# Order of the logit transposes and the third stage's products, and of the high rows' stores, in a long convolution followed by soft mixture-of-experts

## The chip, the cores and the metric

The kernel runs on one core of one Trainium2 chip. The metric is the device time of one execution in microseconds (us), lower being better; where several runs are given, their median is used. Profiles come from one separately profiled execution.

The core has five engines with instruction queues of their own: TensorE (PE in the profile, its weight loads as PEld), VectorE (DVE), ScalarE (ACT), GpSimd (POOL) and SyncE (SP), which here issues nearly all DMA transfers. Each queue is worked off in order; queues wait for each other through semaphores.

## The reference

The input `x` is (8, 5696, 128), the filter `h` is (5696, 128), both float32. The first half is a causal convolution along the 5696 positions, done as a product of Fourier transforms of twice that length:

```python
Xf = np.fft.rfft(x, n=2 * S, axis=1)
Hf = np.fft.rfft(h, n=2 * S, axis=0)
y = np.fft.irfft(Xf * Hf[None], n=2 * S, axis=1)[:, :S, :]
```

The result is taken as 45568 tokens of 128 values. The second half is a soft mixture of experts with 8 experts of 4 slots:

```python
logits = x @ phi                        # (45568, 32)
d = softmax(logits, axis=0)             # dispatch, over the tokens
slot_input = d.T @ x                    # (32, 128)
slot_out[e] = relu(slot_input[e] @ w1[e]) @ w2[e]
c = softmax(logits, axis=1)             # combine, over the slots
out = c @ slot_out                      # (45568, 128)
```

The dispatch softmax runs over all tokens, so no output row can be made before the last token's logits are known; the kernel keeps a running column maximum and rescales a running sum.

## The kernel before

**Transform.** The length is split as 90 x 64 (5696 = 89 x 64), and the filter is treated as a ninth batch, the first one. There are three stages, and between them the data goes to DRAM and comes back in another layout.

- *First stage.* A chunk `c` is four of the 32 column pairs of one batch; a batch has 8 chunks, so there are 72. `load_x` (L184) loads it in two transfers, `fold` (L202) makes its sum and difference on POOL (`comp` 0 and 1), and `first_stage` (L210) multiplies them by a table (L217) into two PSUM banks, which ACT copies to `fst` (L220). SP stores `fst` to the DRAM tensor `f` (L226). The 90 rows of the result are split: `first_low` makes the first 60 for one chunk, two stores of 240 KB; `first_high` makes the last 30 for two chunks at once, in four strips of 32 partitions (strip `o` starts at partition 32 `o`; the order is chunk c-1 comp 0, chunk c-1 comp 1, chunk c comp 0, chunk c comp 1), four stores of 120 KB. `fst` has four buffers.
- *Second stage.* A batch has 12 units. `load_g` (L243) brings one in (`gt`, 512 KB). `stage_b1` (L254) transforms it on PE (L263) into `bt` and multiplies by the filter's spectrum on DVE (L281, L290, giving `yf`). `stage_b2` (L294) transforms back (L305); ACT copies the result to `zst` (L311), and SP stores it to the DRAM tensor `z` (L314). `stage_b2` always works on the unit before the one that `stage_b1` has just done.
- *Third stage.* A pair `T` is two chunks of output; a batch has 4 pairs, so there are 32. `load_pair` (L334) brings it in with five transfers (`zc`, 1.4 MB, one buffer until the tail). `stage_c1` (L348) is a generator with three steps: the first makes two products of four matmuls each (L361, two PSUM banks), ACT copies one (L370) and DVE makes sum and difference with the other (L366, L367). The second makes two more products and copies one to `om` (L374). The third makes the sum and difference again on DVE, and POOL makes the final rows of `y` (L380).

**Experts' front.** For a pair, `stage_c2` transposes `y` (L391), `stage_c3` makes the logits (L400) and copies them to `lt` (L403), and `column_max` (L407) updates the running negative maximum `low` on DVE. `stage_c4` (L425) transposes `lt` on PE (four transposes into one bank, L429), copies the result to `L` (L433) and makes the exponential of `lt` with `low` as the bias (L435), with a second small exponential for rescaling (L440); POOL clears one column (L437), DVE takes the maximum over the slots (L444), and POOL subtracts it (L445). `stage_c5` (L449) transposes the exponentials (L452); `softmax` (L458) and `stage_c6` (L500) finish the combine weights; `dispatch` (L471) adds to the slots' sums.

**Order.** It is written out by hand. A loop runs over time steps `t` from 0 to 80, and in every step the letters of a string are called one after the other; `work_` (L592) says which function a letter stands for. Odd steps use ORDER_E, even steps ORDER_O (in the first nine steps FILL_E and FILL_O) (L566). The engines' queues take the instructions in this order.

In an odd step of ORDER_E: `x` loads a chunk, `X` and `Y` are `first_low` and `first_high`, `f` folds the next chunk, `1` is the first step of `stage_c1` for pair T, `4` is `stage_c4` for pair U = T - 1, `j` and `w` are the second and third step of `stage_c1`, `b` is a unit of the second stage, `5` is `stage_c5` and `s` is `softmax` for U. In an even step of ORDER_O: `z` loads the next pair, `P` loads units, `x`, `X`, `f`, `b` as before, `2`, `3` and `m` are `stage_c2`, `stage_c3` and `column_max` for the pair made in the step before, `6` is `stage_c6`, `d` is `dispatch`.

The first stage ends with step 71. Pair T is in step 27 + 2T, so `stage_c4` first comes in step 29. After step 80 the last pairs follow in straight code (L643 on), then the experts' small products, and last the output (L798 on). This code calls the same functions in an order of its own.

All PSUM banks used by these functions come from `bank()` (L173), a ring of four until the tail: a product can begin when the bank taken four calls earlier has been read.

Of the kernel before, what the change touches and what calls it, by code (L numbers as in the profile page):

```python
# [77 lines left out]
def kernel(  # L78
# [94 lines left out]
    def bank():  # L173
        rings.append(rings.pop(0))
        return rings[-1].tile([P, 512], F32, name="bank", tag="bank")
# [23 lines left out]
    def folded(c, comp):  # L199
        return xf[c % 2 * 2 + comp]  # L200
# [9 lines left out]
    def first_stage(tiles, width):  # L210

        st = apool.tile([P, CH, 2, D], F32, name="fst", tag="fst", bufs=4)
        for G in range(2):
            p = bank()
            for o, (c, comp) in enumerate(tiles):
                k = slice(0, HP) if width == HP else slice(HP, HP + QP)
                nc.tensor.matmul(p[o * width:(o + 1) * width, :], s1[:, comp + G, k],  # L217
                                 folded(c, comp)[:, :, :].rearrange("p n d -> p (n d)"),
                                 start=True, stop=True)
            nc.scalar.activation(st[:, :, G, :],  # L220
                                 p[:, :].rearrange("p (n d) -> p n d", d=D), AF.Copy)
        for o, (c, comp) in enumerate(tiles):
            g, j = divmod(c, NJ)
            n0 = comp * HALF + CH * j
            k0, n = (0, N1A) if width == HP else (N1A, N1 - N1A)
            nc.sync.dma_start(  # L226
                out=fd[g].rearrange("q a r c d -> (q a) (r c d)")[k0:k0 + n, n0 * 2 * D:(n0 + CH) * 2 * D],
                in_=st[o * width:o * width + n, :, :, :].rearrange("k n c d -> k (n c d)"))

    def first_low(c):  # L230
        first_stage([(c, comp) for comp in range(2)], HP)

    def first_high(c):
        first_stage([(c - 1 + i, comp) for i in range(2) for comp in range(2)], QP)
# [328 lines left out]
    for comp in range(2):  # L563
        fold(0, comp)
    wait_b2 = []
    ORDER_E, ORDER_O, FILL_E, FILL_O, XAHEAD = "xXYf14jwb5s", "zPxXfb26db3m", "xYfX14jwb5s", "zPxfXb26db3m", 3  # L566

    for t in range(last_front + 1):
        us = list(units(t))
# [286 lines left out]
```

## Time and profile before

| | |
|---|---|
| time, median of 3 runs | 865.26 us (859.84 to 866.72) |
| the profiled execution | 866.74 us, of which the span is 864.4 us |
| PE busy | 769.7 us (89% of the span) |
| DVE busy | 626.5 us (72%) |
| ACT busy | 437.4 us (51%) |
| POOL busy | 374.8 us (43%) |
| DMA | 271.99 MB, 315 GB/s on average |

The span is the profiled execution from its first to its last instruction. In the profile, L217 is line 217 of the kernel, `bank<-x,s` is what an instruction writes and reads, and the arrow `<-` in a list of waits names what ended an engine's idle time. A matmul's time in the profile includes that of its pipeline, so the sum of single matmuls can be larger than the time they take together: four transposes of 272 ns each are through 0.59 us after they began.

The main loop has a steady part. From about 200 us to 640 us each two steps (one odd, one even) repeat after 20.26 us. Before it, up to 200 us, the third stage is not yet running; between 640 and about 720 us the first stage is over and the loop runs out; then come the last pairs, the experts' products, and from about 800 us the output.

### The profile page before, as it was taken

How to read it: one execution, taken by the hardware profiler on the slowest of the kernel's cores; microseconds unless marked ns; L12 is line 12 of the kernel's file. 1: busy time of each engine (PE TensorE's matmuls, PEld its weight loads, DVE VectorE, ACT ScalarE, POOL GpSimd, SP SyncE). 2: the span in 40 equal slices, each digit the busy share in tenths (PEclk: the TensorE clock that was granted, in tenths of full speed). 3: DMA queues.
4: the chain of work that ended last, by engine and by line, in shares of the span. 5: the costliest groups of instructions: out<-in, count | busy, mean ns of one | idle time of the engine just before them, and what ended most of it. 6: DMA issues, size and time to landing. Idle time of an engine off the chain costs nothing.

```text
span 864.4 us, 20502 instructions
## 1 busy us (share of the span) xinstructions
PE 769.7 (89%) x7796; PEld 374.4 (43%) x7796; DVE 626.5 (72%) x942; ACT 437.4 (51%) x967; POOL 374.8 (43%) x359
## 2 busy tenths in 40 slices
PE   5878888779999999999999999999978878978882
PEld 1222333234444444444444444444444444445882
DVE  3259867658777878887888788877778997973542
ACT  3422344435655655665566556656544545562531
POOL 2133424245556556665566555555533443540000
PEclk9999999989999999999999999999999999997755
DMA  9989999999999999999999999999997797760998
GB/s 294 294 268 308 306 319 342 337 335 331 329 323 343 343 349 318 343 337 340 325 336 345 320 339 330 348 312 335 334 333 264 265 316 277 283 276 8 371 380 327
DMA packets 153243, 271.99 MB, mean 315 GB/s; under 512 B 11878, under 2 KB 110054, under 8 KB 150005
## 3 DMA queue, kind: packets, MB, share of 16 engines
q1 hardware_dynamic: 152571, 270.38, 90.5%
q8 instruction: 62, 1.02, 0.4%
q10 hardware_dynamic: 576, 0.31, 0.1%
q14 instruction: 34, 0.28, 0.1%
HBM read 142.57 MB, written 127.98 MB: 313 GB/s over the span
## 4 chain that ended last, share of the span: by engine, by line
PE 58%; DMA 21%; DVE 12%; SPq 3%; issue 2%; ACT 1%; POOL 1%; DVEq 0%; ACTq 0%; POOLq 0%
PE bank L217 14%; PE bank L361 13%; PE bank L305 8%; PE bt L263 7%; PE bank L391 5%; DMA zc<-z 5%; DMA xc<-in_x_dram 5%; DMA out_dram<-o 5%; PE bank L478 3%; DMA gt<-f 3%; DMA xc<-in_h_dram 2%; DVE yf L290 2%; SPq L342 2%; DVE p L281 2%; DVE bt L281 2%
## 5 line engine op out<-in xcount | busy, mean ns | idle before, releaser
L207 POOL TENSOR_TENSOR x<-xc 128x512 f32<-128x512 f32 x126 | 158.0, 1276 | 245.0 <-PE bank L217 177.0
L217 PE MATMUL bank<-x,s 128*64 128x512 f32 (+1 forms) x1152 | 224.6, 610 | 14.0 <-DVE x L207 9.2
L311 ACT ACTIVATE zst<-bank 128x512 f32<-128x512 f32 (+1 forms) x184 | 98.6, 586 | 184.3 <-PE bank L305 165.1
L220 ACT ACTIVATE fst<-bank 128x512 f32<-128x512 f32 x216 | 127.4, 598 | 106.3 <-PE bank L217 87.6
L281 DVE TENSOR_TENSOR p<-bt,Hi 128x1024 f32<-128x1024 f32 x96 | 111.3, 1160 | 32.7 <-PE bt L263 31.6
L361 PE MATMUL bank<-zc,i 128*64 128x512 f32 x480 | 119.1, 618 | 12.4 <-DMA zc<-z 10.0
L305 PE MATMUL bank<-yf,vt 64*64 64x256 f32 x1440 | 100.8, 387 | 25.7 <-DVE yf L290 25.6
L263 PE MATMUL bt<-gt,wt 64*64 64x256 f32 x1620 | 114.3, 389 | 9.6 <-DMA gt<-f 8.1
L290 DVE TENSOR_TENSOR yf<-bt,p 128x512 f32<-128x512 f32 x192 | 119.4, 663 | 3.3
L217 PEld LDWEIGHTS bank<-x,s 128*64 128x64 f32 (+1 forms) x1152 | 55.8, 124 | 150.3 <-issue 79.9
L281 DVE TENSOR_TENSOR bt<-bt,Hr 128x1024 f32<-128x1024 f32 x96 | 113.0, 1177 | 0.0
L263 PEld LDWEIGHTS bt<-gt,wt 64*64 64x64 f32 x1620 | 54.2, 132 | 84.6 <-issue 33.1
L380 POOL TENSOR_TENSOR y<-y,op 128x512 f32<-128x512 f32 x64 | 77.6, 1212 | 13.4 <-DVE op L366 10.4
L305 PEld LDWEIGHTS bank<-yf,vt 64*64 64x64 f32 x1440 | 56.3, 134 | 57.4 <-issue 23.1
L366 DVE TENSOR_TENSOR y<-bank,y 128x512 f32<-128x512 f32 x32 | 22.1, 692 | 77.3 <-PE bank L361 73.8
L380 POOL TENSOR_TENSOR y<-y,om 128x512 f32<-128x512 f32 x54 | 64.1, 1187 | 2.1
L361 PEld LDWEIGHTS bank<-zc,i 128*64 128x64 f32 x480 | 30.9, 139 | 76.8 <-issue 46.6
L391 PE MATMUL bank<-ident,y 109*128 109x109 f32 x512 | 62.4, 272 | 1.3 <-DVE y L380 1.0
L391 PEld LDWEIGHTS bank<-ident,y 109*128 109x128 f32 x512 | 52.1, 147 | 17.2 <-issue 9.2
L393 ACT ACTIVATE yt<-bank 128x360 f32<-128x360 f32 x128 | 51.0, 490 | 2.4 <-PE bank L391 1.8
L809 PE MATMUL op<-so,cT 32*128 32x128 f32 x704 | 45.9, 379 | 5.7 <-ACT o L818 5.2
L466 POOL TENSOR_TENSOR L<-L,rs 128x512 f32<-128x512 f32 x32 | 33.6, 1051 | 31.1 <-DVE rs L465 20.9
(96 smaller groups left out, 792.0 us busy)
## 6 DMA issues: line engine op xcount, KB each, us to landing
gt<-f SPq DMA_DIRECT2D x99, 512.0 KB
z<-zst SPq DMA_DIRECT2D x88, 512.0 KB
f<-fst SPq DMA_DIRECT2D x144, 240.0 KB
zc<-z SPq DMA_DIRECT2D x30, 1024.0 KB
xc<-in_x_dram SPq DMA_DIRECT2D x64, 320.0 KB
f<-fst SPq DMA_DIRECT2D x144, 120.0 KB
out_dram<-o SPq DMA_DIRECT2D x16, 1024.0 KB
zc<-z SPq DMA_DIRECT2D x90, 128.0 KB
```

The lines of the kernel that those rows point to most:

```text
L207: eng.tensor_tensor(out=folded(c, comp)[:, :, :], in0=t_[:, 0, :, :], in1=t_[:, 1, ::-1, :], op=AL.subtract if comp else AL.add)
L217: nc.tensor.matmul(p[o * width:(o + 1) * width, :], s1[:, comp + G, k], folded(c, comp)[:, :, :].rearrange("p n d -> p (n d)"), start=True ...
L220: nc.scalar.activation(st[:, :, G, :], p[:, :].rearrange("p (n d) -> p n d", d=D), AF.Copy)
L263: nc.tensor.matmul(bt[q * HP:(q + 1) * HP, a, o, :], wt[r, 2 * i + q, :], t_[r, 2 * o + q, :, :].rearrange("p c d -> p (c d)"), start=True ...
L281: nc.vector.tensor_tensor(out=p_, in0=pv, in1=h_, op=AL.mult)
L290: eng.tensor_tensor(out=y_[r, 0:k, c, :], in0=pv[:, :, c, :], in1=pi[r, 0:k, 1 - c, :], op=op_)
L305: nc.tensor.matmul(bz[q][a * HP:(a + 1) * HP, o * 2 * D:(o + 1) * 2 * D], vt[r, i, a, :], y_[r, a * m + o, :, :].rearrange("p c d -> p (c ...
L311: nc.scalar.activation(st[:, 0:m, q, :], bz[q][:, 0:m * 2 * D].rearrange("p (o x) -> p o x", o=m), AF.Copy)
L361: nc.tensor.matmul(p[h_ * HP:(h_ + 1) * HP, :], i1[0:kr, tab, :], t_[0:kr, h_, o, :, q, :], start=True, stop=True)
L380: eng.tensor_tensor(out=part_, in0=part(v, 0), in1=o_[:, :, :], op=sign)
L391: nc.tensor.transpose(p[:, i * TR:(i + 1) * TR], ys[T][0:TR, k * CH + i, 0:D], ident[0:TR, 0:TR])
L393: nc.scalar.activation(yt[:, k * CH:(k + 1) * CH, :, :], of_tokens(p), AF.Copy)
```

## The change

Two lines change.

In `first_stage` the stores of `fst` are issued in a different sequence. The list of strips is sorted by whether the strip's number is odd. For the low rows with two strips this leaves the sequence as it was. For the high rows with four strips it becomes 0, 2, 1, 3, which starts at partitions 0, 64, 32, 96 where it was 0, 32, 64, 96. Each store writes the same bytes to the same place.

In ORDER_E the letters `1` and `4` change places: `stage_c4` of pair U is issued ahead of the first step of `stage_c1` of pair T. The other three strings stay.

```diff
-        for o, (c, comp) in enumerate(tiles):
+        for o, (c, comp) in sorted(enumerate(tiles), key=lambda v: v[0] % 2):
             g, j = divmod(c, NJ)
             n0 = comp * HALF + CH * j
             k0, n = (0, N1A) if width == HP else (N1A, N1 - N1A)
@@
-    ORDER_E, ORDER_O, FILL_E, FILL_O, XAHEAD = "xXYf14jwb5s", "zPxXfb26db3m", "xYfX14jwb5s", "zPxfXb26db3m", 3
+    ORDER_E, ORDER_O, FILL_E, FILL_O, XAHEAD = "xXYf41jwb5s", "zPxXfb26db3m", "xYfX14jwb5s", "zPxfXb26db3m", 3
```

More of the change, by code (lines that the diff above doesn't have):

```diff
@@ L565 @@
     wait_b2 = []
-    ORDER_E, ORDER_O, FILL_E, FILL_O, XAHEAD = "xXYf14jwb5s", "zPxXfb26db3m", "xYfX14jwb5s", "zPxfXb26db3m", 3
+    ORDER_E, ORDER_O, FILL_E, FILL_O, XAHEAD = "xXYf41jwb5s", "zPxXfb26db3m", "xYfX14jwb5s", "zPxXfb26db3m", 3
     for t in range(last_front + 1):
```

## The prediction

> **What bounds the kernel now.** I read the page's slices first, then the stretches, then who TensorE waits for, then single pairs in order of time.
>
> ```profile
> PE   5878888779999999999999999999978878978882
> DMA  9989999999999999999999999999997797760998
> ```
>
> Slices of 21.6 us. From slice 10 to 29 both PE and DMA stand at 9. The table of stretches says how full they are (columns: length, then busy us of each engine, granted clock, DMA share, GB/s):
>
> ```profile
> 100.00:200.00 100.00, 81.11 (x767) 32.86 (x764) 68.00 (x80) 42.51 (x77) 35.41 (x29) 0.95 0.99 332
> 200.00:640.00 440.00, 431.70 (x4462) 201.79 (x4462) 352.67 (x541) 261.91 (x596) 254.18 (x237) 1.00 0.97 334
> 640.00:720.00 80.00, 66.96 (x720) 36.76 (x720) 68.29 (x106) 36.81 (x85) 27.46 (x28) 0.89 0.84 289
> ```
>
> 100 to 200 us is the transfers' stretch (0.99 busy, PE at 81%). 200 to 640 us is PE's: 431.7 of 440 us busy, so 8.3 us is all that any edit can win there without taking PE work away. From 640 us (no first stage left) VectorE carries it, 68.3 of 80 us. What PE waits for between 200 and 650 us (us in total, times, longest):
>
> ```profile
> PE bank L361 <- DMA zc<-z: 5.3, 6, 2.6
> PE bank L305 <- DVE yf L290: 3.5, 6, 1.8
> PE bank L361 <- DMA f<-fst: 1.2, 1, 1.2
> PE bank L361 <- ACT fst L220: 0.9, 1, 0.9
> ```
>
> The waits ahead of L361 are what the first edit aims at. One of them in order of time (start, us, work):
>
> ```profile
> 477.74 3.79 PE L217 MATMUL bank<-x,s 128*64 128x512 f32 x24
> 482.18 1.94 PE L361 MATMUL bank<-zc,i 128*64 128x512 f32 x8 [0.66 <-DMA zc<-z]
> 484.05 0.66 PE L429 MATMUL bank<-ident,lt 128*128 128x128 f32 x4
> 484.64 1.94 PE L361 MATMUL bank<-zc,i 128*64 128x512 f32 x8
> ```
>
> The four transposes behind the products need only `lt`, there since the step before; they take 0.59 us on PE (484.05 to 484.64). Lastly a pair after 640 us, where nothing stands between L400, which makes `lt`, and these transposes:
>
> ```profile
> 664.30 1.94 PE L361 MATMUL bank<-zc,i 128*64 128x512 f32 x8
> 664.63 0.49 ACT L403 ACTIVATE lt<-bank 128x360 f32<-128x360 f32 x1
> ...
> 665.43 0.60 ACT L370 ACTIVATE y<-bank 128x512 f32<-128x512 f32 x1 [0.30 <-PE bank L361]
> 666.17 0.66 PE L429 MATMUL bank<-ident,lt 128*128 128x128 f32 x4
> ...
> 667.76 0.61 ACT L435 ACTIVATE dt<-lt,low 128x360 f32<-128x360 f32 x1 [0.30 <-DVE low L416]
> 667.78 0.69 DVE L366 TENSOR_TENSOR y<-bank,y 128x512 f32<-128x512 f32 x1
> ...
> 670.42 0.69 DVE L367 TENSOR_TENSOR om<-bank,om 128x512 f32<-128x512 f32 x1
> ```
>
> Here L403 runs under the first products, and DVE, not PE, ends last: L305 later waits 2.67 us for `yf`.
>
> **What the Trainium skill says.** (1) "SBUF — State Buffer", section 'Can I just issue two DMAs to hit both halves?': two transfers at once, at partitions 0 and 64, gave +6% over one. (2) "DMA: Bandwidth & Descriptors", 'Rules for kernel authors', says of transfers to disjoint halves "Don't bother — they serialize". The trace agrees as far as it goes: put in order of time, the 4 KB packets of the high stores take 177 ns on average and those of the low stores, whose two transfers already lie in opposite halves, 176 ns. (3) "TensorE: Matmul & The Clock Gate", 'Part 4: PE-mode transpose', gives about 275 ns for a 128x128 transpose in a kernel (bf16). L429 shows 272 ns each, but four overlap to 0.59 us; I use the 0.59.
>
> **Part 1: the order of products and transposes (32 pairs have L429; the 26 that the loop issues change, 22 before 640 us and 4 after; the written-out tail does not).** Nothing is added. On PE the four L429 move ahead of sixteen L361; on ACT L433, L435 and L440 move ahead of L370; on DVE L444 moves ahead of the first L366 and L367. POOL's (L437, L445, then L380) and SP's orders stay. In the ring of four PSUM banks the block's fifth, the last L361's, now waits for L433 and not L370; either is done over a microsecond before.
>
> *While PE is full (22 pairs).* Both orders keep PE 0.59 + 2 x 1.87 = 4.3 us, so without a wait nothing is won. Where `zc` is late, PE does the 0.59 us in the wait. The gaps ahead of L361 are 0.41, 0.68, 0.86, 0.66, 0.35, 0.58 and 1.24 us; of each at most 0.59 is filled: 0.41 + 0.35 + 0.58 + 4 x 0.59 = 3.7 us. Does it stay won? `zc` may simply come at its own time again. After the wait at 400.9 us the transfers run dry (share 0.83 from 411 to 420 us) because SP waits for work that PE paces, so they should move up with it; at 97% I allow four fifths: -2.9 us.
>
> What could eat it is ACT. Count from the start of this block: the last L220 copy ends at 0.81. L433, L435 and L440 follow each other at 0.5 us, so L370 starts near 2.0 and not 1.12, ends at 2.6, when the second L361 bank is full too (2.6 against 2.04). DVE then folds from 2.65 to 4.1. The next fold starts at 4.51 today and waits for the last L361 at 4.39. So 0.4 us of slack is left: cost nothing, with that as its cover.
>
> *The first pair after 640 us.* L361 waits 2.61 us for `zc`, `lt` and `low` being ready (642.9 and 644.4). The transposes, 1.1 us here at a lowered clock, go into the wait: -1.1 us. The block took 6.0 us where others take 4.4, clock granted 0.81 around it; if a shorter idle time avoids that, up to 1 us more, which I don't count.
>
> *The other three.* The transposes must wait for L403: L400's end to L403's end is 0.8 us, plus 0.1, so PE idles 0.9 us (now covered by L361). Behind it, L435 on ACT waits for `low` (3.46 after the first L361 today), then L440, so L370 starts about 4.05 and not 1.13. On DVE, behind the column maximum ending at 3.56: L444 to 4.25, a wait for L370 to 4.65, then four folds of 0.70 us: 7.5 against 6.82 today. So +0.7 us on the chain that ends last, three times: +2.1 us. Bounds: 0 (if a later wait takes it up) and 1.0 each.
>
> **Part 2: the stores.** The same four transfers of 120 KB, in the same place of SP's order, in the sequence of rows 0, 64, 32, 96. Whoever needs the data or the buffer waits for all four, whose bytes go through one queue. From below: the high stores' packets lie 17 ns over the median 159; 36 groups x 120 packets x 17 ns / 16 engines = 4.7 us, if all of that vanished and all of it were on the path. The page's +6% gives an estimate of 4.1 us: groups last some 1.9 us, 36 x 1.9 x 0.06. From above: the low stores, already alternating, are within 1 ns, 0.3 us by the same working; I keep 1 us. I take 0, since the low stores show no advantage.
>
> **Sum.** -2.9 - 1.1 + 2.1 + 0 = -1.9 us. The profiled execution took 866.7 us (span 864.4, 2.3 around it): it would be 864.8. Against the median of the runs, 865.26, that is 863.4. The three runs lie 6.9 us apart, so a measurement of this kernel tells about 1% (8.7 us) from no change, and this isn't.
>
> **The rivals.**
> - *All of it pays* (0.14): the waits are filled whole (-3.7), the clock holds at 645 us (-2.1), the drain's 2.1 us is absorbed, the stores gain the 4.1 us: 865.3 - 9.9 = 855.4. For: 100 to 200 us is bound by transfers. Against: 22 of the 36 groups lie where PE sets the pace, and packets are near their floor already.
> - *The copy in ACT's queue* (0.12): L370 behind L433, L435 and L440 makes L366 and L367 late in the 22 full pairs too. It decides once L370 slips 0.4 us beyond my 2.0. At 0.75 us beyond, 0.35 x 22 = +7.7; the drain at 1.0 each, +3.0; the waits won are lost in it; -1.1 stays: 865.3 + 9.6 = 874.9. For: DVE's `yf` comes just before PE wants it (L305 at 9.67 after the block's start, DVE done at 9.52). Against: ACT is busy 60%, and its times repeat to 0.01 us from pair to pair.
> - *It does not do what it says* (0.14): `zc` comes when the transfers let it, so each wait grows by what was filled. Then -1.1 + 2.1 = +1.0: 866.3.
> - My forecast (0.60): 863.4, 859 to 868 on its own.
>
> **Numbers.** Of the first rival somewhat over half lies beyond 1%, of the second under half: faster 0.08, within 1% 0.87, slower 0.05. The range 857.5 to 870 leaves out the far halves of these two and the outer edge of the runs' own scatter.
>
> **What would show it.** Right: in the list of waits, L361 <- `zc` and `fst` between 200 and 640 us falls from 4.8 to about 1.5 us, PE's busy time there stays, and the period of two steps stays 20.26 us; after 650 us, L429 waits 0.9 us for L403 three times, and the last fold of a pair ends about 0.7 us later after L400. The packets of the high stores keep their 177 ns. Wrong: a period over 20.3 us with DVE's L366 waiting for L370 (second rival); L361's waits as long as before (third); a GB/s over 340 between 100 and 200 us with that stretch shorter by 2 us or more (first). A wait of L305 for `yf` in every pair would break the slack I rely on.

## The result

Over 20 runs of each the changed kernel takes 865.42 us (858.63 to 871.75) and the kernel before 865.84 us (859.7 to 872.31): a ratio of 0.9992, 95% interval 0.9973 to 1.0012, that is -2.3 to +1.0 us. Nothing that can be measured. (The ratios in this document leave out the few executions that fell into the chip's slower state, here one of the changed kernel, so they can differ a little from those of the medians.)

A correction first. The changed kernel has a third difference, which the description and the diff above miss: FILL_O, the order of the even steps 0 to 8, reads `zPxXfb26db3m` and not `zPxfXb26db3m`. There the fold of the next chunk (on DVE in these steps, in step 8 on POOL) and `first_low` (PE, ACT, SP) change places. They use different engines, and with and without this difference every engine gets the same instructions in the same order with the same waits. So it changes nothing that runs, and the two parts treated above are what there is.

### The profile page after: what moved, and what is told of

Its sections match the earlier page's. It is cut to its first block, busy times and chain, and to the rows that moved or that the text cites. A ratio compares the mean times of both kernels' runs of the same rounds, so it can differ in the third digit from the quotient of the medians.

```text
span 863.6 us, 20505 instructions
## 1 busy us (share of the span) xinstructions
PE 764.5 (89%) x7796; PEld 378.0 (44%) x7796; DVE 627.4 (73%) x942; ACT 435.5 (50%) x967; POOL 374.7 (43%) x359
## 4 chain that ended last, share of the span: by engine, by line
PE 54%; DMA 21%; DVE 14%; SPq 4%; issue 2%; ACT 2%; POOL 1%; DVEq 0%; ACTq 0%; POOLq 0%
PE bank L217 12%; PE bank L361 11%; PE bank L305 7%; PE bt L263 7%; PE bank L391 6%; DMA zc<-z 6%; DMA xc<-in_x_dram 5%; DMA out_dram<-o 4%; DMA gt<-f 3%; PE bank L478 3%; DVE yf L290 3%; DVE p L281 2%; DVE bt L281 2%; DMA xc<-in_h_dram 2%; SPq L342 2%
## 5 line engine op out<-in xcount | busy, mean ns | idle before, releaser
L217 PE MATMUL bank<-x,s 128*64 128x512 f32 (+1 forms) x1152 | 224.8, 615 | 10.9 <-DVE x L207 8.3
L361 PE MATMUL bank<-zc,i 128*64 128x512 f32 x480 | 113.4, 614 | 15.1 <-DMA f<-fst 7.7
L263 PE MATMUL bt<-gt,wt 64*64 64x256 f32 x1620 | 113.9, 388 | 12.2 <-DMA gt<-f 10.8
L305 PE MATMUL bank<-yf,vt 64*64 64x256 f32 x1440 | 99.9, 384 | 25.1 <-DVE yf L290 25.0
L217 PEld LDWEIGHTS bank<-x,s 128*64 128x64 f32 (+1 forms) x1152 | 55.7, 124 | 146.7 <-issue 80.9
L263 PEld LDWEIGHTS bt<-gt,wt 64*64 64x64 f32 x1620 | 54.2, 132 | 87.9 <-issue 38.9
L305 PEld LDWEIGHTS bank<-yf,vt 64*64 64x64 f32 x1440 | 56.0, 133 | 56.0 <-issue 20.1
L361 PEld LDWEIGHTS bank<-zc,i 128*64 128x64 f32 x480 | 35.3, 139 | 72.4 <-issue 51.2
L391 PE MATMUL bank<-ident,y 109*128 109x109 f32 x512 | 62.8, 273 | 1.3 <-DVE y L380 1.0
L391 PEld LDWEIGHTS bank<-ident,y 109*128 109x128 f32 x512 | 52.4, 147 | 17.0 <-issue 10.8
L444 DVE TENSOR_REDUCE rm<-L 128x16 f32<-128x512 f32 x32 | 21.9, 685 | 40.8 <-POOL x L207 37.5
```

The lines of the kernel that those rows point to most:

```text
L263: nc.tensor.matmul(bt[q * HP:(q + 1) * HP, a, o, :], wt[r, 2 * i + q, :], t_[r, 2 * o + q, :, :].rearrange("p c d -> p (c d)"), start=True ...
L305: nc.tensor.matmul(bz[q][a * HP:(a + 1) * HP, o * 2 * D:(o + 1) * 2 * D], vt[r, i, a, :], y_[r, a * m + o, :, :].rearrange("p c d -> p (c ...
L361: nc.tensor.matmul(p[h_ * HP:(h_ + 1) * HP, :], i1[0:kr, tab, :], t_[0:kr, h_, o, :, q, :], start=True, stop=True)
L391: nc.tensor.transpose(p[:, i * TR:(i + 1) * TR], ys[T][0:TR, k * CH + i, 0:D], ident[0:TR, 0:TR])
```

## The profile after

The table of stretches of the changed kernel (columns as above: length, busy us of PE, PEld, DVE, ACT, POOL, granted clock, DMA share, GB/s):

```profile
100.00:200.00 100.00, 80.22 (x765) 32.91 (x766) 68.04 (x81) 43.44 (x79) 35.15 (x30) 0.97 0.97 328
200.00:640.00 440.00, 428.24 (x4464) 204.93 (x4464) 354.17 (x541) 259.31 (x594) 253.49 (x235) 1.00 0.97 335
640.00:720.00 80.00, 65.36 (x722) 37.08 (x716) 66.96 (x104) 36.85 (x86) 27.55 (x28) 0.91 0.83 290
```

Between 200 and 640 us PE is busy for 3.5 us less than before (428.2 against 431.7), with as many matmuls (4464 against 4462), and idle for 3.5 us more. The transfers stand at 0.97 as before. What PE waits for in this stretch (us in total, times, longest), first L361 in the kernel before:

```profile
PE bank L361 <- DMA zc<-z: 2.7, 5, 0.7
PE bank L361 <- DMA f<-fst: 1.2, 1, 1.2
PE bank L361 <- ACT fst L220: 0.9, 1, 0.9
```

Then the changed kernel:

```profile
PE bank L305 <- DVE yf L290: 3.5, 6, 1.8
PE bank L361 <- DMA zc<-z: 3.3, 3, 1.7
PE bank L361 <- DMA f<-fst: 2.5, 3, 1.1
PE bank L361 <- ACT dn L440: 1.3, 1, 1.3
PE bank L361 <- ACT L L433: 0.8, 1, 0.8
PE bank L361 <- ACT fst L220: 0.2, 1, 0.2
```

L361 waited 4.8 us before; now it waits 8.1 us, and that after the transposes have filled the first 0.59 us of each gap. (L440 and L433 had ended when the wait ended, and L361 reads nothing of `f`; what these matmuls still lack is `zc`.) One of these waits in order of time:

```profile
477.11 3.79 PE L217 MATMUL bank<-x,s 128*64 128x512 f32 x24
480.83 0.66 PE L429 MATMUL bank<-ident,lt 128*128 128x128 f32 x4
482.28 3.65 PE L361 MATMUL bank<-zc,i 128*64 128x512 f32 x16 [0.79 <-DMA f<-fst]
```

PE comes 0.6 us earlier than before to the end of L217 (480.83 against some 481.5), does the transposes in the gap as forecast, and the products begin at 482.28 where they began at 482.18. `zc` came when it came.

And a pair after 640 us:

```profile
662.88 0.81 PE L400 MATMUL bank<-yt,phi 128*32 128x360 f32 x8
...
663.96 0.49 ACT L403 ACTIVATE lt<-bank 128x360 f32<-128x360 f32 x1
664.50 0.66 PE L429 MATMUL bank<-ident,lt 128*128 128x128 f32 x4 [0.80 <-ACT lt L403]
...
667.09 0.60 ACT L435 ACTIVATE dt<-lt,low 128x360 f32<-128x360 f32 x1 [1.30 <-DVE low L416]
...
667.68 0.58 ACT L370 ACTIVATE y<-bank 128x512 f32<-128x512 f32 x1
...
668.29 0.69 DVE L366 TENSOR_TENSOR y<-bank,y 128x512 f32<-128x512 f32 x1 [0.50 <-ACT y L370]
...
670.34 0.69 DVE L367 TENSOR_TENSOR om<-bank,om 128x512 f32<-128x512 f32 x1
```

The queue of events is the one forecast: L429 waits 0.80 us for L403, L435 waits for `low`, L370 stands behind it, DVE waits for L370. L400 began at 662.88, so the last fold ends 8.15 us after it (671.03); before, it ended 7.55 us after (663.56 to 671.11).

## The experiments

Theory T says that the steady part goes at the pace of the transfers: whatever PE saves, the next wait for `zc` grows by it (the third rival). Theory F says what the forecast said: filled waits stay won, and then something else must have lost them.

**The order alone.** Only the first part of the change:

```diff
-    ORDER_E, ... = "xXYf14jwb5s", ...
+    ORDER_E, ... = "xXYf41jwb5s", ...
```

> Part 1 alone: stage_c4 ahead of the first step of stage_c1 in the odd steps, stores as before. Theory T (transfers pace the steady part, so L361's wait for zc grows by whatever PE saves): a full pair takes 20.10 us and not 20.26, the waits ahead of L361 between 200 and 640 us add up to about 8 us and not 4.8, and the distance from the L361 of step 29 to the last L400 before 645 us stays at 443.5 us within 1 us; time within 0.3% of before. Theory F (the filled waits stay won, as in the forecast, and something else took them away in the changed kernel, the stores being the candidate): that distance falls by 3 us or more and the time by 0.3% or more.

Measured: 865.53 us against 864.84, ratio 0.9996 (0.9972 to 1.0019). A full pair takes 20.10 to 20.11 us, the distance is 444.8 us (before 443.5, changed kernel 443.1). So no stores are needed to lose the gain; F fails here. The distance is 1.4 us more than before and not within 1 us as T had it. It scatters by that much from one execution to another: in the profiled executions with the full load it is 443.5 us twice with the old order (before, and the stores alone below) and 443.1, 444.8 and 443.4 us with the new (changed, this one, and the kernel with the drain put back, below).

**The stores alone.**

```diff
-        for o, (c, comp) in enumerate(tiles):
+        for o, (c, comp) in sorted(enumerate(tiles), key=lambda v: v[0] % 2):
```

> Part 2 alone: the four stores of the high rows in the sequence of strips 0, 2, 1, 3. Theory N (the sequence means nothing): time within 0.3% of before, a full pair 20.26 us, the stretch 100 to 200 us at the same 332 GB/s within 2%. Theory H (opposite halves help or hurt the transfers): the first L361, at 177.15 us before, moves by over 2 us, since up to there transfers set the pace.

Measured: 864.85 us against 864.84, ratio 0.9990 (0.9965 to 1.0014); the first L361 at 176.83 us (177.15 before). Stretches of this kernel:

```profile
100.00:200.00 100.00, 78.97 (x777) 32.72 (x770) 68.36 (x80) 42.47 (x77) 35.58 (x29) 0.98 0.99 335
200.00:640.00 440.00, 431.90 (x4465) 202.37 (x4468) 352.64 (x542) 261.94 (x596) 253.99 (x236) 1.00 0.97 334
```

335 GB/s in the transfers' stretch against 332, and the packets of the high stores take 175 ns on average against 177. Theory N holds: the sequence means nothing that shows here. The interval, -3.0 to +1.2 us, leaves out the 4.1 us of the first rival.

**Fewer bytes, old and new order.** Half of the input load is left out in both kernels, nothing else:

```diff
             v = bass.AP(tensor=v.tensor, offset=v.offset,
-                        ap=[v.ap[0], [gap * D, 2], [1, CH * D]])
+                        ap=[v.ap[0], [1, CH * D]])
             nc.sync.dma_start(
-                out=t_[X0 + r.start:X0 + r.stop, :, :, :].rearrange("p s n d -> p s (n d)"), in_=v)
+                out=t_[X0 + r.start:X0 + r.stop, 0, :, :].rearrange("p n d -> p (n d)"), in_=v)
```

> Kernel before, with half of the input load left out: of every chunk only the first of the two column groups of x and h is brought in, the other half of xc stays zero, so the convolution is computed from half of its input. That is 178 KB of some 3.3 MB per step, 5.5%; no other instruction changes. Theory T (transfers pace the steady part): the waits ahead of L361 from 200 us on fall to near 0 and each two steps take 20.26 us; the part up to the first L361 is shorter by 5 us or more; time about 1% less than before. Theory F (the waits ahead of L361 are a latency, not a shortage of transfer capacity): the waits stay at 4 us or more.

> The changed kernel with the same half of the input load left out (the other half of xc stays zero). Theory T: with transfers out of the way PE's saving shows: two steps take 20.10 us, and from step 29 to the last L400 before the loop runs out it needs 22 x 0.155 = 3.4 us less than the light kernel before; in total about 3 us less than that, the drain's 3 x 0.6 us against it. Theory F: no difference between the two light kernels.

Measured: 844.82 us (843.86 to 845.16, 4 runs) for the old order and 842.92 us (842.02 to 844.80, 4 runs) for the new, with 864.84 for the kernel before beside them. Taking 5% of the bytes away made the kernel 2.3% faster (medians). The two light kernels' runs overlap, so what the order is worth is read from the traces. All that PE waits for between 200 and 600 us, in the light kernel of the old order and then in that of the new:

```profile
PE bank L305 <- DVE yf L290: 1.8, 5, 0.4
```

```profile
PE bank L305 <- DVE yf L290: 1.8, 5, 0.4
```

No wait for `zc` is left in either, at a DMA share of 0.93 and 0.94. The number of transfers that SP issues is the same as with the full load; only their bytes are fewer. Now the new order shows what it is worth: eight steps take 79.98 us and not 80.59 (three times 20.10 or 20.11 and one 19.66, against three times 20.26 and one 19.81), 0.15 us a pair. T holds and F falls. From step 29 to the last L400 of the full part the new order needs 435.7 us against 438.2, 2.5 us less and not 3.4. In the last two steps of this part it is 1.3 us slower (21.11 us against 19.82): L305 and L391 run slowly (1.82 and 2.61 us, in the old order 1.09 and 1.89) after a wait for `yf` that both kernels have (1.78 and 1.77 us).

**Where the 0.15 us comes from.** The new order leaves all sixteen L361 of a pair together; the old one put L429 between them. A block of the light kernel, old order, then new:

```profile
446.07 1.94 PE L361 MATMUL bank<-zc,i 128*64 128x512 f32 x8
447.94 0.66 PE L429 MATMUL bank<-ident,lt 128*128 128x128 f32 x4
448.52 1.94 PE L361 MATMUL bank<-zc,i 128*64 128x512 f32 x8
450.39 1.09 PE L263 MATMUL bt<-gt,wt 64*64 64x256 f32 x16
```

```profile
444.42 0.65 PE L429 MATMUL bank<-ident,lt 128*128 128x128 f32 x4
445.00 3.65 PE L361 MATMUL bank<-zc,i 128*64 128x512 f32 x16
448.58 1.09 PE L263 MATMUL bt<-gt,wt 64*64 64x256 f32 x16
```

4.32 us from the first L361 to L263, against 4.16 from L429 to L263. In single records two neighbouring pairs of L361 begin 0.43 us apart; at a change of operation it is 0.52, and the first pair after it takes 0.47. To test whether changes of operation are what costs, one kernel has one more than the old order. The letter `1` goes from ORDER_E, and `4` passes the first step of `stage_c1` to `stage_c4`, which calls it after two of its four transposes (cut):

```diff
         p = bank()
         for i in range(CH):
+            if i == CH // 2 and between is not None:
+                between()
             nc.tensor.transpose(...)
```

> The changed kernel with half of the input load left out (the other half of xc stays zero), and two of the four transposes ahead of the first eight L361, two between these and the second eight: the same matmuls, two more changes of operation in PE's row than in the changed kernel and one more than before. Theory C (a change of operation costs PE about 0.155 us): two steps take 20.41 us in the steady part. Theory P (what counts is only where the transposes stand relative to the copies on ACT and the folds on DVE): 20.26, as with the old order, or 20.10, as with the new.

Measured: 848.49 us (2 runs). Its block, from the profile (L431 is the transposes' line here):

```profile
448.45 0.44 PE L431 MATMUL bank<-ident,lt 128*128 128x128 f32 x2
448.82 1.94 PE L361 MATMUL bank<-zc,i 128*64 128x512 f32 x8
450.69 0.44 PE L431 MATMUL bank<-ident,lt 128*128 128x128 f32 x2
451.05 1.94 PE L361 MATMUL bank<-zc,i 128*64 128x512 f32 x8
452.92 1.09 PE L263 MATMUL bt<-gt,wt 64*64 64x256 f32 x16
```

4.47 us, and full pairs take 20.40 or 20.41 us throughout. Theory C is confirmed to 0.01 us: 20.10, 20.26 and 20.41 for one, two and three changes inside this part of PE's row. What it is in a change that costs is not separated: with the operation the shape of the tiles changes too, and inside L217, where the low rows' 128x64 give way to the high rows' 128x32, the starts are 0.52 us apart as well (light changed kernel, 442.04 to 442.56 us), so a change of shape may be enough.

**The drain put back.** The new order as long as there is a first stage, the old one in steps 73 to 79 (the stores as before with the full load, as in the changed kernel with the light one):

```diff
+        ORDER_D = ORDER_E.replace("41", "14") if t >= NA else ORDER_E
-        for c_ in ((ORDER_E if full else FILL_E) if t % 2 else (ORDER_O if full else FILL_O)):
+        for c_ in ((ORDER_D if full else FILL_E) if t % 2 else (ORDER_O if full else FILL_O)):
```

> The order change in the steps with a first stage only (t below 72); in the odd steps 73 to 79 the products stay ahead of the transposes as before, and the stores are as before. If the drain's cost is what it seems in the traces (the last fold of a pair comes 8.15 us after L400 began and not 7.55), the three pairs from step 75 on go back to 7.55, 1.8 us in all: 0.2% below the order change alone, which these runs cannot tell from no change; the trace must show it. If it is not, the three pairs stay at 8.15.

> The changed kernel with half of the input load left out (the other half of xc stays zero) and, in steps 73 to 79, the old order of products and transposes. The light kernels scatter by little over 1 us, so the drain's cost can be timed: against 842.9 us of the light changed kernel about 1.8 us less (841.1) if each of the three last pairs costs 0.6 us; no difference if something later takes it up.

Measured with full transfers: 865.33 us against 865.25, ratio 1.0006 (0.9984 to 1.0028). With light ones: 840.47 us (839.35 to 843.27, 4 runs), 2.4 us under the light changed kernel, in another set of runs, and near the 841.1 us expected. This was meant as the version that beats both; under full transfers it doesn't, within what can be measured.

In the traces the last fold ends 7.61, 7.74 and 7.87 us after L400 with full transfers, and 7.56, 7.56 and 7.64 with light ones: the order's delay is gone, as expected; the rest goes with a later start of L361. But the traces give more than expected. From one L400 to the next, for the three pairs from step 75 on (us):

| kernel | first | second | third | sum |
|---|---|---|---|---|
| before | 18.86 | 18.74 | 18.20 | 55.80 |
| stores alone | 18.86 | 18.74 | 18.20 | 55.80 |
| changed | 19.46 | 18.01 | 18.52 | 55.99 |
| order alone | 19.48 | 18.02 | 18.52 | 56.02 |
| drain put back | 17.48 | 17.60 | 18.25 | 53.33 |
| light, drain put back | 17.42 | 17.43 | 18.21 | 53.06 |
| light, old order | 17.42 | 18.87 | 19.34 | 55.63 |
| light, changed | 19.45 | 18.02 | 18.62 | 56.09 |

The kernel before, the one with the stores alone, the light one of the old order and the two with the drain put back all run these three pairs in the old order, yet their sums reach from 53.06 to 55.80 us. In the first two columns there are four kinds of pair: with the old order some 17.4 to 17.6 or 18.7 to 18.9 us, with the new order 18.0 or 19.5. The order costs 0.6 us in either kind (17.42 to 18.02, 18.87 to 19.46), as the fold's delay says. The other 1.4 us are TensorE's clock. The second pair before, and then the first and the second pair in the changed kernel:

```profile
693.72 1.98 PE L305 MATMUL bank<-yf,vt 64*64 64x256 f32 x16 [2.67 <-DVE yf L290]
695.63 2.32 PE L391 MATMUL bank<-ident,y 109*128 109x109 f32 x16
```

```profile
674.77 1.09 PE L305 MATMUL bank<-yf,vt 64*64 64x256 f32 x16 [2.54 <-DVE yf L290]
675.80 3.17 PE L391 MATMUL bank<-ident,y 109*128 109x109 f32 x16
```

```profile
694.23 1.09 PE L305 MATMUL bank<-yf,vt 64*64 64x256 f32 x16 [2.54 <-DVE yf L290]
695.25 1.89 PE L391 MATMUL bank<-ident,y 109*128 109x109 f32 x16
```

From L305's start to the end of L391 these take 4.23, 4.20 and 2.91 us; the clock granted is 0.72 from 693 to 699 us before, 0.72 from 674 to 680 us in the changed kernel, and 1.00 there from 693 to 699 us. With the drain put back, L361 waits about 1 us in each of the three pairs (0.87, 1.00 and 1.13), and L305 in the first two then 1.77 and not 2.67:

```profile
672.79 1.09 PE L305 MATMUL bank<-yf,vt 64*64 64x256 f32 x16 [1.77 <-DVE yf L290]
673.82 1.89 PE L391 MATMUL bank<-ident,y 109*128 109x109 f32 x16
```

and the clock is 1.00 from 660 to 700 us. So all of the 1.4 us that the first pair gains over the kernel before (18.86 to 17.48) are matmuls at the full clock. It is tempting to say that two shorter waits spare PE what one long one costs. The record speaks against the wait's length alone: the two waits of 2.54 us above end one way and the other; in the light kernel of the old order a wait of 2.66 us is followed by the full clock (L391 in 1.89 us at 653.70 us) and one of 1.80 us by a lowered one (2.85 us at 671.12 us). What decides it is open, and with it whether other executions fall the same way. So the gain of the kernel with the drain put back is the order's only as far as the 0.6 us a pair go; in the light kernels' traces (56.09 to 53.06 us) 1.4 of the 3.0 us are the clock in the first pair, so that 840.47 us came near the expected 841.1 does not show that the order alone was worth the 1.8 us.

## Why the prediction was right, and where it was not

The forecast, 863.4 us and most likely no change that can be measured, held; the sum behind it did not hold in every term. The time can't tell the forecast's -1.9 us from the third rival's +1.0, as the interval of -2.3 to +1.0 us holds both, so the terms are judged by the traces. Of -2.9, -1.1 and +2.1 us these show -0.4, -0.3 and +0.2: three terms too large, of opposite signs, so that their errors cancelled in part, which is luck.

- *Filled waits stay won, -2.9 us.* This failed, at the sentence that the transfers "should move up" with PE. The filling happened, but from step 29 to step 72 the changed kernel took 443.1 us and the kernel before 443.5. The third rival, with a chance of 0.14, described this part. I had taken the dip of the DMA share to 0.83 after a wait as room for the transfers to move up; with the full load they didn't, and only with 5% of the bytes gone did a saving of PE's reach the end of this part. A stretch with PE at 98% and DMA at 97% has two limits, and I named one.
- *PE's work stays the same (0.59 + 2 x 1.87).* Wrong by 0.15 us a pair: one change of operation fewer. 22 pairs make 3.4 us, PE's busy time fell by 3.5. With the full load the waits swallowed it with the rest. Without that the forecast of the full pairs at 20.26 us would have been right; it was 20.10.
- *Slack of 0.4 us behind the copy on ACT.* Held: the fold of `om` starts 0.12 us after the last L361 as before, and L305's waits for `yf` are the same 3.5 us. The second rival did not come about.
- *First pair after 640 us, -1.1 us.* From its L400 to the next, 22.24 became 21.97 us: -0.3. The transposes went into the wait (1.65 us were left of it). But `zc` came no earlier (L361 began at 644.83 us, before at 644.75) while PE's L400 was 0.4 us earlier, and the lowered clock stayed: the sixteen products took 5.35 us where others take 3.65, and the block from the first L361 to L263 fell from 5.90 to 5.28 us only.
- *The other three pairs, +2.1 us.* The chain was right link by link: 0.80 us of wait for L403 (forecast 0.9), the last fold 0.60 us later (forecast 0.7). The sum was not: 55.80 to 55.99 us, +0.2. At the same clock the delay is worth its 0.6 us a pair; but in the changed kernel's trace the second pair ran at the full clock, where the kernel before had a lowered one, and that gave back 1.3 us. No run shows that the order brought this about.
- *Stores, 0.* Held, as the low stores had suggested. On this the pages of the Trainium skill that were quoted are borne out as far as they go: "Don't bother"; the +6% of the other page did not appear, in transfers that queue behind others anyway. (The bound from below, 36 x 120 x 17 ns / 16, is 4.6 us and not 4.7; nothing rests on it.)

## What to carry to other kernels

Here TensorE was 98% and the transfers 97% busy, and a wait removed on one came back as the next wait for the other. Where two resources are this full, take a few per cent of the other's work away for one run, and see whether the edit is worth anything then. Matmuls of one kind in one piece saved TensorE time: each change to another group in its row cost 0.15 us here. And in a stretch where TensorE idles and its clock is lowered now and then, compare pairs at the same clock before a saving or delay of half a microsecond is put down to an edit: the clock was worth 1.4 us a pair here.

## What was not expected of the hardware

The change of operation on TensorE: 0.15 us, the same from one to two and from two to three changes. The clock after a wait: full after 2.66 us and lowered after 1.80 us in one trace. The scatter: kernels with the full load spread over 10 to 13 us in 20 runs (859.7 to 872.3 before), those with half the input load over 1 to 4 us in 4 runs, so most of it seems to come with saturated transfers, though 4 runs are few. And some 5.5% fewer bytes in each step with a first stage took 20 us off: 12 us of them came before the first L361 (177.15 to 165.57 us), 5 us in the steady part, the rest between the two and after it.
